# Dealing the rows of a weight to the partitions in another order, and its small vector with it

## Chip, cores, metric

One core of a Trainium2 chip. The metric is the device time of one execution in microseconds (us). All arithmetic and all data are float32.

## The reference

The kernel is one decode step (one token for each of two batch rows, D = 512) of a transformer block with adaptive layer norm. Cut to what matters here:

```python
mod = (silu(c) @ w_mod).reshape(2, 6, 1, 512)        # c: (2, 512), w_mod: (512, 3072)
sa, ca, ga, sb, cb, gb = six rows of mod
h = layernorm(x) * (1 + ca) + sa                     # x: (2, 1, 512)
x = x + ga * attention(h)                            # wq: (512, 4096), 8 kv heads, last 4096 of 32768 keys
h = layernorm(x) * (1 + cb) + sb
x = x + gb * (silu(h @ w1) @ w2)
```

The product of `silu(c)` with `w_mod` comes first: all that follows needs it, the query projection included. It sums over the 512 rows of `w_mod`. In which order they are summed, and which row lies in which partition, is free as long as `c` is dealt in the same order.

## The kernel before

**Memory.** All large operands are read once, in the order in which they are used, through one ring of eight slots of 16 KB in each partition (`slots`, function `stream`). A transfer takes one or more slots, and its issue has to wait until the work that read the former contents is done. All large transfers are issued by SyncE (SP) and so lie in one hardware queue, in this order: `w_mod` (three slots), `x`, `wq` (four slots), then for eight steps a pair of heads of the key cache and of the value cache (two slots each), then `wo`, `w1` and `w2`. The first pair of the key cache and the second take the slots of `w_mod` and one that has not been used, so SP issues them when the last matmuls on `w_mod` are done.

**`w_mod`.** `load_runs(w_mod, 4, 0, 4)` puts rows 4p to 4p+3 into partition p: each partition reads 48 KB that lie together in memory, and 128 such blocks make up the matrix.

**`c`.** The condition vector lies in the tile `xc` (half `c_sp`, 128 partitions by 128 elements, set to zero first). For each of the two batch rows the 512 numbers are cut into four pieces of 128, and each piece goes to the first or the 17th partition of a group of 32. ScalarE (ACT) issues four transfers for it, each with two pieces of 512 bytes, in a hardware queue of its own. VectorE (DVE) then transposes it in blocks of 32 by 32 (`turned`, line 255), which gives `cT`: partition r of step k holds element 4r + k. `silu_exp` and a product make `scT` out of it.

**The head of the kernel, in order.** DVE: zero `xc`, transpose `c` (this waits for the four transfers), SiLU, then small constants, then the layer norm's statistics of `x`, the modulated `h_a`, and its transpose `hq_T`. PE: 64 matmuls into `m_a` and `m_sp` (lines 269 and 272) with `scT` as weights and `w_mod` as data; then 64 matmuls of the query projection `q` (line 302) on `wq`; then the steps of the attention. Every engine works through its own list in order, so what stands behind the transpose of `c` on DVE waits with it.

**Steps of the attention.** In each step DVE transposes a pair of key heads (line 361), PE makes the scores (line 374), softmax follows, and PE weighs the values (line 448). SP issues the next transfers as slots come free (line 82).

Of the kernel before, what the change touches and what calls it, by code (L numbers as in the profile page):

```python
# [13 lines left out]
P = 128  # L14
B, D = 2, 512
# [8 lines left out]
def adaln_block(  # L24
# [19 lines left out]
    nc = tc.nc  # L44
# [16 lines left out]
    def const(shape, name):  # L61
        return consts.tile(shape, F32, name=name)

    def bank(tag, name):
        return (psum1 if tag in "CO" else psum).tile([P, 512], F32, tag=tag, name=name)
# [4 lines left out]
    def stream(n=1):  # L70
        i = turn_of[0]
        if n % 2 == 0:
            i += -i % n
        turn_of[0] = i + n
        return slots[:, i % RING : i % RING + n, :].rearrange("p s e -> p (s e)")
# [12 lines left out]
    def load_runs(w, per, lo, hi):  # L88

        e = w.shape[1]  # L90
        n = -(-(hi - lo) * e // 4096)
        t = stream(n)[:, : (hi - lo) * e].rearrange("p (q e) -> p q e", e=e)
        nc.sync.dma_start(t, w.rearrange("(p q) e -> p q e", q=per)[:, lo:hi, :])
        return t
# [3 lines left out]
    xc = const([P, 2, P], "xc")  # L98
    x_sp, c_sp = xc[:, 0, :], xc[:, 1, :]
    nc.vector.memset(xc, 0.0)  # L100
    wm = load_runs(w_mod, 4, 0, 4)
    rows8 = lambda t: t.rearrange("(ab r) m -> ab r m", r=16)[:, 0, :]
    for b in range(B):
        for lo in (0, 2):
            nc.scalar.dma_start(
                c_sp.rearrange("(g y) m -> g y m", g=4)[lo : lo + 2, 16 * b, :],
                c[b].rearrange("(g m) -> g m", m=P)[lo : lo + 2],
            )
    nc.sync.dma_start(rows8(x_sp), x2.rearrange("b (g m) -> g b m", m=P))  # L109
    wqt = load_runs(wq, 4, 0, 4)  # L110
# [108 lines left out]
    def silu_exp(t, name, shape):  # L219

        e = once.tile(shape, F32, tag="silu", name=name)
        nc.vector.tensor_scalar(e, t, -1.0, 87.0, op0=ALU.mult, op1=ALU.min)
        nc.scalar.activation(e, e, AF.Exp)
        nc.vector.tensor_scalar(e, e, 1.0, None, op0=ALU.add)
        nc.vector.reciprocal(e, e)
        return e
# [26 lines left out]
    def turned(t, name):  # L253
        o = const([P, 4, 32], name)
        nc.vector.transpose(o, t.rearrange("p (m k) -> p k m", k=4))  # L255
        return o

    cT = turned(c_sp, "cT")
    sg = silu_exp(cT, "sgc", [P, 4, 32])
    scT = const([P, 4, 32], "scT")  # L260
    nc.vector.tensor_mul(scT, cT, sg)  # L261
# [315 lines left out]
    for q in range(28):  # L577
        g = q % 4
# [80 lines left out]
    for tt in range(WIDE):  # L659
        g = tt % 4  # L660
# [7 lines left out]
    y = bank("D", "acc_y")[:, :P]  # L668
# [13 lines left out]
    for tt in range(11, T2):  # L682
        for h in range(2):
            for g in range(4):
                lo = g * P + h * H
# [46 lines left out]
```

## Time and profile before

| What | Value |
|---|---|
| median of 3 runs | 235.59 us (235.44 to 235.62) |
| the profiled execution | span of 233.7 us from its first to its last instruction; 1.9 us of the median lie outside it |
| busy: PE, DVE, ACT, POOL | 161.1, 115.6, 28.5, 10.5 us |
| read from memory | 97.53 MB, 417 GB/s over the span |
| packets of SP's queue | 3768, 97.1% of 16 engines' span |
| packets of ACT's queue | 16 |

Times in rows of the trace are in us from the span's start. In a row of the timeline stand start, duration, engine, line, operation, output and inputs; an "SPq" or "ACTq" row is the issue of a transfer, not the transfer itself. A view of the transfers by window gives, for that window, how many packets started, how many of them were under 512 bytes, and how many belonged to each queue: q1 is SP's, q10 is ACT's. The DMA share is the mean busy share of the 16 DMA engines; in a short window it can pass 1.00, since a packet counts where it starts.

### The profile page before, as it was taken

The page shows a single profiled execution, that of the slowest core. Times are in us where ns is not written, and L with a number is a line of the kernel's source. Part 1 is how long each engine was busy: PE and PEld are TensorE (multiplying, and loading weights), DVE is VectorE, ACT ScalarE, POOL GpSimd, SP SyncE. Part 2 cuts the span into 40 slices and gives each one's busy share as a digit, 9 for nine tenths or more (in the row PEclk, how much of TensorE's full clock was granted, in tenths as well). Part 3 has the DMA queues.
Part 4 walks back from the last instruction along what each step waited for, and adds up shares of the span by engine and source line. Part 5 has one row for each costly group of instructions (what it writes and reads, how often), then busy time and mean ns, then how long its engine had stood idle before and what let it go on. Part 6 is the DMA issues. An engine that isn't in the chain of part 4 may idle for free.

```text
span 233.7 us, 2571 instructions
## 1 busy us (share of the span) xinstructions
PE 161.1 (69%) x1070; PEld 43.3 (19%) x1070; DVE 115.6 (49%) x179; ACT 28.5 (12%) x64; POOL 10.5 (4%) x35
## 2 busy tenths in 40 slices
PE   0004916859577839797598749759759779789684
PEld 0001401201111111211120201202112122324222
DVE  0007240278894758695197089259559540101232
ACT  2000210000311120120210201111020120102020
POOL 2004710000000000000000000000000000000000
PEclk9999985979999977999979999988997997999999
DMA  7998998999999999999999999999999999989991
GB/s 269 446 542 359 404 494 359 446 444 421 415 421 449 446 437 415 426 426 446 449 437 409 418 437 449 449 421 412 426 444 449 443 421 437 463 367 437 424 404 57
DMA packets 3794, 97.68 MB, mean 418 GB/s; under 512 B 432, under 2 KB 456, under 8 KB 968
## 3 DMA queue, kind: packets, MB, share of 16 engines
q1 hardware_dynamic: 3768, 97.53, 97.1%
q8 instruction: 8, 0.13, 0.2%
q14 instruction: 2, 0.02, 0.0%
q10 hardware_dynamic: 16, 0.00, 0.0%
HBM read 97.53 MB, written 0.00 MB: 417 GB/s over the span
## 4 chain that ended last, share of the span: by engine, by line
DMA 60%; issue 18%; DVE 14%; PE 6%; POOL 0%; SPq 0%; POOLq 0%; ACT 0%
DMA slots<-in_A_k_cache_dram 22%; DMA slots<-in_A_wq_dram 15%; DMA slots<-in_A_v_cache_dram 12%; DMA slots<-in_B_w_dram 12%; DVE kT L361 11%; PE o L448 2%; PE q L302 2%; DVE zp L420 1%; PE acc_yw L661 1%; DVE xp L418 1%; PE qr L323 0%; PE acc_y L671 0%; DVE qT L315 0%; POOL qg L319 0%; SPq L109 0%
## 5 line engine op out<-in xcount | busy, mean ns | idle before, releaser
L361 DVE STREAM_TRANSPOSE kT<-slots 128x1024 f32<-128x1024 f32 x64 | 73.7, 1212 | 23.7 <-DMA slots<-in_A_k_cache_dram 23.6
L374 PE MATMUL s<-kT,qbd 128*32 128x512 f32 x256 | 68.6, 693 | 19.1 <-DVE kT L361 18.0
L448 PE MATMUL o<-slots,ptb 128*32 128x512 f32 x256 | 30.8, 624 | 2.1 <-DMA slots<-in_A_v_cache_dram 2.1
L374 PEld LDWEIGHTS s<-kT,qbd 128*32 128x32 f32 x256 | 9.6, 113 | 68.4 <-DVE kT L361 63.4
L269 PE MATMUL m_a<-slots,scT 128*32 128x256 f32 x32 | 4.4, 506 | 20.5 <-DVE scT L261 20.5
L302 PE MATMUL q<-slots,hq_T 128*32 128x512 f32 x64 | 8.3, 680 | 7.0 <-DMA slots<-in_A_wq_dram 7.0
L448 PEld LDWEIGHTS o<-slots,ptb 128*32 128x32 f32 x256 | 8.1, 114 | 17.9 <-issue 17.8
L404 ACT COPY bias<-bp 128x1 f32<-128x1 f32 x8 | 1.3, 159 | 77.0 <-PE bp L402 77.0
L384 DVE TENSOR_REDUCE mx<-s 128x1 f32<-128x512 f32 x8 | 5.5, 691 | 9.6 <-PE s L374 9.6
L565 PE MATMUL junk<-quad,id 128*32 128x512 f32 x22 | 10.2, 595 | 0.0
L420 DVE TENSOR_TENSOR zp<-xp,quarter 128x1024 f32<-128x1024 f32 x8 | 9.8, 1225 | 0.2
L435 ACT ACTIVATE ptb<-pT,odd 128x256 f32<-128x256 f32 x16 | 6.7, 472 | 25.6 <-PE pT L427 25.6
L255 DVE STREAM_TRANSPOSE cT<-xc 128x128 f32<-128x128 f32 x1 | 0.4, 401 | 16.7 <-DMA xc<-in_c_dram 16.7
L427 PE MATMUL pT<-zp,mix 128*32 128x256 f32 x64 | 5.7, 428 | 3.6 <-DVE zp L420 3.5
L458 ACT COPY ob<-o 128x512 f32<-128x512 f32 x8 | 4.7, 585 | 26.1 <-PE o L448 26.1
L272 PE MATMUL m_sp<-slots,scT 128*32 128x512 f32 x32 | 7.4, 738 | 0.0
L386 PE MATMUL mT<-ident,mx 128*1 128x128 f32 x16 | 3.0, 270 | 6.3 <-DVE mx L384 6.3
L315 DVE STREAM_TRANSPOSE qT<-q 128x512 f32<-128x512 f32 x2 | 1.4, 717 | 11.7 <-PE q L302 10.2
L418 DVE STREAM_TRANSPOSE xp<-pr 128x512 f32<-128x512 f32 x8 | 5.5, 686 | 3.4 <-ACT pr L406 3.4
L579 PE MATMUL acc_o<-slots,oTn 128*32 128x512 f32 x56 | 6.2, 593 | 0.7 <-DMA slots<-in_A_wo_dram 0.7
L466 PE MATMUL o_all<-ob,selh 128*64 128x128 f32 x64 | 6.0, 316 | 0.8 <-ACT ob L458 0.8
L550 DVE COPY acc_o_sb<-acc_o 128x256 f32<-128x256 f32 x1 | 0.4, 425 | 12.4 <-ACT acc_o_sb L549 12.4
(140 smaller groups left out, 93.8 us busy)
## 6 DMA issues: line engine op xcount, KB each, us to landing
slots<-in_A_k_cache_dram SPq DMA_DIRECT2D x8, 4096.0 KB, 27.4
slots<-in_A_v_cache_dram SPq DMA_DIRECT2D x8, 4096.0 KB, 27.6
slots<-in_w_mod_dram SPq DMA_DIRECT2D x1, 6144.0 KB, 17.1
slots<-in_A_wo_dram SPq DMA_DIRECT2D x1, 6144.0 KB
slots<-in_B_w_dram SPq DMA_DIRECT2D x1, 2688.0 KB
slots<-in_A_wo_dram SPq DMA_DIRECT2D x1, 2048.0 KB, 29.5
slots<-in_B_w_dram SPq DMA_DIRECT2D x1, 2048.0 KB
slots<-in_B_w_dram SPq DMA_DIRECT2D x1, 896.0 KB
```

The lines of the kernel that those rows point to most:

```text
L272: nc.tensor.matmul(m_sp[r, :], scT[:, k, :], cd[:, g], start=(k == 0), stop=(k == 3))
L302: nc.tensor.matmul(q_ps[n][32 * g : 32 * g + 32, :], hq_T[:, k, :], wv[:, n, g], start=(k == 0), stop=(k == 3),)
L361: inorder(nc.vector.transpose(kT[s, j][:, 32 * c : 32 * c + 32, :], kt[s].rearrange("p (n j r) -> p j n r", j=4, r=32)[:, j, 32 * c : 32 * ...
L374: inorder(nc.tensor.matmul(s_ps[s][r : r + 32, :], qbd[h // 4][:, h % 4, b, j, :], kT[s, j][:, 32 * c : 32 * c + 32, e:32:2], start=(j == ...
L418: inorder(nc.vector.transpose(xp, pr[s]))
L420: inorder(nc.vector.tensor_mul(zp, xp[:, None, :, 0:16].to_broadcast([P, 4, 16, 16]), quarter[:, :, None, None].to_broadcast([P, 4, 16, 16 ...
L427: inorder(nc.tensor.matmul(tp[32 * i : 32 * i + 32, :], mix.rearrange("p v e -> p (v e)"), zp.rearrange("p y t x -> p (y t) x")[:, :, 4 * ...
L435: inorder(nc.scalar.activation(ptb[s % 2][:, :, e, :], tp.rearrange("p (w z) -> p w z", z=16), AF.Copy, scale=odd[:, e : e + 1],))
L448: inorder(nc.tensor.matmul(o_ps[s][r : r + 32, :], ptb[s % 2][:, w].rearrange("p e z -> p (e z)"), vt[s].rearrange("p (c w m f d) -> p c f ...
L466: inorder(nc.tensor.matmul(o_all[r : r + 64, :], selh[:, m, lo : lo + 2 * HQ], o_sb[s][:, m * DH : (m + 1) * DH], start=(s == 0 and m < 2) ...
L565: inorder(nc.tensor.matmul(junk[0:32, :], id4, quad.rearrange("p m y -> p (m y)"), start=True, stop=True,))
L579: inorder(nc.tensor.matmul(acc[32 * g : 32 * g + 32, :], oTn[:, q, :], wot[q], start=(q < 4), stop=(q >= 24),))
```

## The change

Partition 8j + i now receives block 16i + j of `w_mod` (a block is four rows, 48 KB), for i below 8 and j below 16; before, partition p received block p. `c` has to follow: what was one run of 128 numbers for a partition becomes eight runs of 16, each from another place of the vector. The four transfers of `c` stay four, with the same destinations, and so does the number of bytes. The transpose of `c` reads its tile in a permuted order, so that `cT` matches the new rows. Nothing else is touched: on every engine the same instructions follow each other in the same order.

```diff
-    wm = load_runs(w_mod, 4, 0, 4)
+    wm = stream(3)[:, : 24 * D].rearrange("p (q e) -> p q e", e=6 * D)
+    nc.sync.dma_start(
+        wm.rearrange("p q e -> p (q e)"),
+        w_mod.rearrange("(i j q) e -> j i (q e)", i=8, j=16),
+    )
     rows8 = lambda t: t.rearrange("(ab r) m -> ab r m", r=16)[:, 0, :]
     for b in range(B):
         for lo in (0, 2):
             nc.scalar.dma_start(
-                c_sp.rearrange("(g y) m -> g y m", g=4)[lo : lo + 2, 16 * b, :],
-                c[b].rearrange("(g m) -> g m", m=P)[lo : lo + 2],
+                c_sp.rearrange("(g y) (i a) -> g y i a", g=4, i=8)[lo : lo + 2, 16 * b],
+                c[b].rearrange("(i g a) -> g i a", i=8, g=4)[lo : lo + 2],
             )
...
-    cT = turned(c_sp, "cT")
+    cT = const([P, 4, 32], "cT")
+    nc.vector.transpose(
+        cT.rearrange("p k (y i) -> p k y i", i=8),
+        c_sp.rearrange("p (i y k) -> p k y i", y=4, k=4),
+    )
```

## The prediction, made before the changed kernel ran

> **What bounds the kernel now.** I read the page first: its slices, its queues, and the costliest groups.
>
> ```profile
> span 233.7 us, 2571 instructions
> ...
> q1 hardware_dynamic: 3768, 97.53, 97.1%
> ...
> q10 hardware_dynamic: 16, 0.00, 0.0%
> ...
> L255 DVE STREAM_TRANSPOSE cT<-xc 128x128 f32<-128x128 f32 x1 | 0.4, 401 | 16.7 <-DMA xc<-in_c_dram 16.7
> ...
> slots<-in_w_mod_dram SPq DMA_DIRECT2D x1, 6144.0 KB, 17.1
> ```
>
> SP's queue keeps the 16 DMA engines busy for 97.1% of the span, and it carries all bytes that matter. So the time is the length of that queue plus what stands before and behind it. The windows of the whole kernel (the last two columns are DMA share and GB/s) show whether it ever runs dry:
>
> ```profile
> 6.00:18.00 12.00, 0.00 (x0) 0.00 (x0) 0.12 (x1) 0.00 (x0) 0.00 (x0) 1.00 1.11 481
> 18.00:37.00 19.00, 9.81 (x68) 3.34 (x68) 7.96 (x31) 2.44 (x4) 7.94 (x23) 0.90 0.96 414
> 37.00:77.00 40.00, 30.47 (x166) 6.76 (x170) 23.96 (x29) 4.51 (x11) 0.47 (x2) 0.92 1.00 432
> 77.00:117.00 40.00, 29.55 (x186) 7.05 (x178) 27.06 (x33) 5.82 (x15) 0.49 (x2) 0.91 1.00 432
> 117.00:157.00 40.00, 30.18 (x173) 6.64 (x173) 25.36 (x29) 4.72 (x12) 0.00 (x0) 0.94 1.00 432
> 157.00:197.00 40.00, 32.48 (x206) 8.66 (x208) 24.18 (x30) 5.37 (x14) 0.00 (x0) 0.89 1.02 437
> 197.00:228.00 31.00, 26.17 (x202) 9.11 (x194) 5.04 (x22) 4.01 (x6) 0.00 (x0) 1.00 0.97 416
> ```
>
> It doesn't: the share is 1.00 within the rounding of packets from 6 us to 228 us. Two things follow. A microsecond in which this queue stands empty is lost for good, as no later stage has slack to win it back. And there is little rate to gain while it is full. So the question is whether the change makes the queue faster, or makes it run dry. What could make it run dry is in the head, in the timeline:
>
> ```profile
> 0.73 0.38 SPq L93 DMA_DIRECT2D slots<-in_w_mod_dram  x1
> ...
> 1.16 2.62 ACTq L105 DMA_DIRECT2D xc<-in_c_dram  x4
> ...
> 1.93 0.58 SPq L93 DMA_DIRECT2D slots<-in_A_wq_dram  x1
> ...
> 17.88 0.40 DVE L255 STREAM_TRANSPOSE cT<-xc 128x128 f32<-128x128 f32 x1 [16.75 <-DMA xc<-in_c_dram]
> ...
> 20.51 1.08 PE L269 MATMUL m_a<-slots,scT 128*32 128x256 f32 x8 [20.51 <-DVE scT L261]
> ...
> 29.08 1.84 SPq L82 DMA_DIRECT2D slots<-in_A_k_cache_dram  x2
> ...
> 30.69 0.40 DVE L255 STREAM_TRANSPOSE hq_T<-h_a 128x128 f32<-128x128 f32 x1
> ...
> 37.29 8.34 PE L302 MATMUL q<-slots,hq_T 128*32 128x512 f32 x64 [6.97 <-DMA slots<-in_A_wq_dram]
> ```
>
> The four transfers of `c`, 4 KB in all, are issued by 3.78 and are seen at 17.88: 14 us for 4 KB. From there runs a chain: SiLU, the matmuls on `w_mod`, their slots come free, and SP issues the first key transfers at 29.08. `wq` lands at 37.16 (issued at 1.93, 35.23 us on the chain of waits); until then the queue lives on `wq`.
>
> ```profile
> 1.93 35.23 DMA slots<-in_A_wq_dram
> 37.15 0.14 issue
> ```
>
> So `c` has a slack of about 8 us before the queue runs dry. Why `c` takes 14 us is seen in the transfers by window, here from 6.0 to 7.9, from 7.9 to 9.7, from 9.7 to 11.5 and from 17.0 to 17.6 us:
>
> ```profile
> DMA packets 20, 0.89 MB, mean 466 GB/s; under 512 B 0, under 2 KB 2, under 8 KB 2
> ...
> q10 hardware_dynamic: 2, 0.00, 0.2%
> ...
> DMA packets 18, 0.79 MB, mean 437 GB/s; under 512 B 2, under 2 KB 2, under 8 KB 2
> ...
> q10 hardware_dynamic: 2, 0.00, 0.1%
> ...
> DMA packets 17, 0.74 MB, mean 410 GB/s; under 512 B 0, under 2 KB 2, under 8 KB 2
> ...
> q10 hardware_dynamic: 2, 0.00, 0.2%
> ...
> DMA packets 44, 0.92 MB, mean 1538 GB/s; under 512 B 20, under 2 KB 30, under 8 KB 30
> ...
> q10 hardware_dynamic: 4, 0.00, 0.8%
> ```
>
> ACT's queue gets two packets in each 1.8 us, and their sizes alternate: two of 512 bytes, then two under 512 bytes, then two of 512 bytes. I read this as two engines that take one packet of `c` after each 48 KB packet of `w_mod`: first a data packet, a turn later the packet that reports the completion. Sixteen packets are eight data runs and eight completions, so a transfer of two runs goes to two engines with one run each, and a run is a packet. Eight turns at 1.8 us are the 14 us.
>
> **The change part by part.** *The runs of `c`.* Each transfer has two partitions as before, hence two engines, but eight runs of 64 bytes for each. An engine gets 4 x (8 + 1) = 36 packets instead of 8. By one packet for each turn, 6 go beside the `w_mod` packets until 17.0, 1 to 4 beside the small packets of 17.0 to 17.6 (completion of `w_mod`, `x`), 8 beside the `wq` packets (64 KB, eight for each engine) and 1 beside the completion of `wq`. That makes 16 to 19. The other 17 to 20 find SP's queue empty and run through alone. So `c` lands when `wq` has landed, plus a remainder: 37.16 in place of 17.88.
>
> The remainder: two packets took 0.2% of 16 engines in 1.9 us, which is 0.06 us, so 0.03 us for each. About 12 more of them than before lie in front of the end of `wq` (0.36 us), and about 18 behind it (0.55 us). The lower bound is nothing; as upper bound I take 0.1 us for each behind it (1.8 us), since in the last window the four packets of `c` pass beside others within 0.6 us. I take the row's 0.03, which is for the same queue.
>
> *The issue of `w_mod`.* Its source pattern gets one level more, like that of the key cache, whose issues take longer in the rows of the tile `slots` up to 50 us (min/median/max in ns):
>
> ```profile
> L82 SPq DMA_DIRECT2D slots<-in_A_k_cache_dram x3: 535/546/599, 29.1 to 45.7; - x3
> L93 SPq DMA_DIRECT2D slots<-in_w_mod_dram x1: 377/377/377, 0.7 to 0.7; - x1
> ```
>
> That is +0.16 us on the start of the queue (bounds: 0 and 0.22), and nothing hides it.
>
> *The order of the reads.* The queue already moves 432 GB/s where it is full, and `w_mod` moves at that pace but for its start. `wq` (8192 KB) lands 19.33 us behind `w_mod` (0.73 + 17.1 = 17.83), which is 2.36 us for 1024 KB; by that pace the 6144 KB of `w_mod` need 14.5 us of its 17.1. The other 2.6 us are what a transfer into an empty queue costs before and behind its bytes. All that another order can save lies in there. The first sixteen packets, one for each engine, start between 1.7 and 3.0 us:
>
> ```profile
> DMA packets 16, 0.79 MB, mean 605 GB/s; under 512 B 0, under 2 KB 0, under 8 KB 0
> ```
>
> So about 1.0 of the 2.6 pass before any packet, whatever the order. Taken as 0; bounds: a gain of 1.6 us and, the other way, a start as much worse.
>
> *The transpose of `c`.* Same 128x128 elements, one level more in the source: 0.40 us, taken as unchanged; bounds: 0 and 0.4 us more, should the level double it.
>
> *The sum.* `cT` starts at 37.16 + 0.16 + 0.36 + 0.55 = 38.2 in place of 17.88, 20.3 us later. Nothing on DVE, PE or POOL can go ahead of it: the constants, the statistics of `x` and the matmuls all stand behind it or need it. So the 11.2 us from 17.88 to the issue at 29.08 follow unchanged and SP issues the keys at 49.4. This transfer now meets an empty queue and pays the 2.6 us, plus 0.16 which its issue takes longer than that of `w_mod`: 49.4 + 2.76 = 52.2. Before, its bytes followed those of `wq` directly, from 37.16. The queue has lost 52.2 - 37.16 = 15.0 us, and all of it reaches the end. The span has 233.7 us against the median of 235.59; the 1.9 us outside it stay. 235.59 + 15.0 = 250.6 us.
>
> What lies beside it: `hq_T` starts at 30.69 + 20.3 = 51.0 and `q` ends some 9 us behind, at about 60, while the first keys land at 52.2 + 9.4 (4096 KB at 2.36) = 61.6. `q` stays hidden, and `wq`'s slots come free before the queue, which by then holds two pairs of keys, is done with them. If `q` were later by 2 us, the scores would start late, but the queue would not notice.
>
> **The rivals.** *Several runs in one turn.* If an engine takes all that one `c` transfer has for it in a turn, `c` costs no more turns than before. The threshold is low: the queue runs dry only if the key issue comes after 37.16 - 2.76 = 34.4, so `cT` after 23.2. With three packets in a turn, 36 packets need 12 turns, which end with the second `wq` packet at about 17.4 + 2 x 2.4 = 22.2 (16 packets of `wq` in 19.33 / 8 = 2.4 us): just no loss. With two, 18 turns end with `wq` all the same. The time then is 235.59 + 0.16 = 235.75. Against it speaks that a data packet and its own completion, which lie behind one another in the same queue, took turns 1.8 us apart. [...]
>
> *Faster: the new order pays at the start.* If neighbouring blocks end the slow start of `w_mod`, and `c` isn't late, the queue ends earlier by up to 1.6 - 0.16 = 1.4 us; half of it gives 234.9. It decides only together with the first rival, since a queue that waits for `c` gains nothing from an earlier `w_mod`. The full rate of 432 GB/s from 37 us on, with the key cache read in its own order, speaks against a large part.
>
> *The remainder is dear.* If each of the 18 lone packets takes 0.1 us, `cT` starts 1.25 us later: 251.9.
>
> **How the numbers follow.** 0.2% of the time, 0.47 us, is about what can be told from no change. I give the forecast 0.86, the dear remainder 0.03, several runs in a turn 0.07 (of which 0.06 within 0.2% and 0.01 faster by luck of the start), and the faster start with it 0.04. So: faster 0.05, same 0.06, slower 0.89. The range stays with the slow cases, since the others hold only 0.11. Its lower end takes no remainder and no small packets in front (-0.9), and 1.0 instead of 2.6 us for the empty queue (-1.6), with some more for a head that runs faster while the DMA engines are idle: 247.8. Its upper end takes the dear remainder, 0.4 for the transpose and some for the start: 252.6.
>
> **What would show it.** In the changed kernel's profile the DMA slices drop to nothing for one or two slices of 5.84 us at about 38 to 51 us; ACT's queue shows 72 packets in place of 16, two in each 1.8 us and then in each 2.4 us; `cT` starts at about 38 and the idle time before it is about 37 us on `c`; SP issues the first keys at about 49. The forecast is wrong if `cT` still starts near 18 us, and its size is wrong if the empty stretch isn't near 15 us or if a later window makes up for it.

## The result, and the profile after

The changed kernel takes 264.3 us (median; 263.94 to 265.5) against 235.58 us (235.35 to 235.62) of the kernel before, run beside it: a ratio of 1.1237, 95% interval 1.122 to 1.1254. The sign was right, the size was not: 250.6 us had been forecast, in a range up to 252.6. The loss is 28.7 us in place of 15.0. The profile is of the run of 265.5 us.

The page of the changed kernel shows two lean stretches at the start, where one had been expected:

```profile
span 263.7 us, 2571 instructions
...
DMA  9899979700999999999999999999999999989992
GB/s 209 172 216 239 279 318 477 318 0 25 385 462 399 467 408 432 435 432 442 418 450 408 462 413 445 423 427 447 418 455 409 447 423 460 447 370 430 431 418 101
...
q10 hardware_dynamic: 72, 0.00, 0.0%
...
L263 DVE STREAM_TRANSPOSE cT<-xc 128x128 f32<-128x128 f32 x1 | 0.4, 394 | 52.1 <-DMA xc<-in_c_dram 52.1
...
slots<-in_w_mod_dram SPq DMA_DIRECT2D x1, 6144.0 KB, 33.1
```

A slice is 6.6 us here. Slices 9 and 10 hold almost no transfer: that is the empty queue of the forecast. But the first five slices are busy and still move only 172 to 279 GB/s, and `w_mod` lands 33.1 us after its issue, not 17.1. A DMA share near 1 beside half the rate means that each packet takes twice as long; a share alone would have hidden it. The windows (share and GB/s are the last two columns) set the stages apart, first `w_mod`, then `wq`, then the empty queue, then all the rest up to 226 us:

```profile
6.00:30.00 24.00, 0.00 (x0) 0.00 (x0) 0.00 (x0) 0.00 (x0) 0.00 (x0) 1.00 1.01 211
34.00:52.00 18.00, 0.00 (x0) 0.00 (x0) 0.00 (x0) 0.00 (x0) 0.00 (x0) 1.00 0.94 408
53.00:65.00 12.00, 9.18 (x65) 3.37 (x68) 5.76 (x24) 1.85 (x3) 7.21 (x21) 1.00 0.00 0
66.00:226.00 160.00, 121.22 (x728) 28.06 (x732) 101.99 (x123) 20.78 (x53) 1.70 (x6) 0.91 1.00 431
```

At 211 GB/s a 48 KB packet takes 3.7 us on each of 16 engines; the trace's packets of `w_mod` behind the first round have 3.54 to 3.85 us, before the change nearly all 1.815. From 66 us on the kernel runs at its old rate, so nothing is won back. The timeline shows the head:

```profile
0.73 0.69 SPq L102 DMA_DIRECT2D slots<-in_w_mod_dram  x1
...
53.19 0.39 DVE L263 STREAM_TRANSPOSE cT<-xc 128x128 f32<-128x128 f32 x1 [52.06 <-DMA xc<-in_c_dram]
...
55.82 1.08 PE L277 MATMUL m_a<-slots,scT 128*32 128x256 f32 x8 [55.82 <-DVE scT L269]
...
64.49 1.84 SPq L82 DMA_DIRECT2D slots<-in_A_k_cache_dram  x2
...
66.56 7.07 PE L310 MATMUL q<-slots,hq_T 128*32 128x512 f32 x64 [0.83 <-DVE hq_T L259]
```

`c` is seen 49.3 us after its last issue (at 3.91), and the chain of waits now leads through it instead of through `wq`:

```profile
3.39 49.68 DMA xc<-in_c_dram
```

How the 72 packets of `c` went is in the transfers by window, from 9 to 32, 32 to 33, 34 to 52 and 52 to 53 us:

```profile
q10 hardware_dynamic: 12, 0.00, 0.1%
...
q10 hardware_dynamic: 10, 0.00, 0.9%
...
q10 hardware_dynamic: 14, 0.00, 0.1%
...
q10 hardware_dynamic: 36, 0.00, 2.4%
```

That is 6 turns for each of two engines beside `w_mod`, 5 beside small packets, 7 beside `wq` (an eighth falls into the last window), and the rest in a row once SP's queue is empty. That is the count of the forecast, turn by turn, with 5 beside the small packets where it had 1 to 4. What the forecast had not seen is the half rate of `w_mod`.

### The profile page after: what moved, and what is told of

Read it like the earlier page. It is cut to its first block, busy times and chain, and to the rows that moved or that the text cites. A ratio compares the mean times of both kernels' runs of the same rounds, so it can differ in the third digit from the quotient of the medians.

```text
span 263.7 us, 2571 instructions
## 1 busy us (share of the span) xinstructions
PE 160.9 (61%) x1070; PEld 42.8 (16%) x1070; DVE 115.6 (44%) x179; ACT 28.5 (11%) x64; POOL 10.5 (4%) x35
## 2 busy tenths in 40 slices
DMA packets 3850, 97.68 MB, mean 370 GB/s; under 512 B 496, under 2 KB 512, under 8 KB 1024
## 4 chain that ended last, share of the span: by engine, by line
DMA 60%; issue 17%; DVE 13%; PE 8%; ACTq 1%; POOL 0%; ACT 0%; POOLq 0%; DVEq 0%
DMA slots<-in_A_k_cache_dram 19%; DMA xc<-in_c_dram 19%; DMA slots<-in_B_w_dram 11%; DMA slots<-in_A_v_cache_dram 11%; DVE kT L369 10%; PE m_sp L280 2%; PE q L310 1%; PE o L456 1%; PE m_a L277 1%; DVE zp L428 1%; ACTq L109 1%; PE acc_yw L669 1%; DVE xp L426 0%; DVE sgc L229 0%; PE acc_y L679 0%
## 5 line engine op out<-in xcount | busy, mean ns | idle before, releaser
L382 PE MATMUL s<-kT,qbd 128*32 128x512 f32 x256 | 70.5, 731 | 20.6 <-DVE kT L369 19.7
L456 PE MATMUL o<-slots,ptb 128*32 128x512 f32 x256 | 29.1, 595 | 2.3 <-DMA slots<-in_A_v_cache_dram 2.3
L277 PEld LDWEIGHTS m_a<-slots,scT 128*32 128x32 f32 x32 | 1.2, 125 | 56.6 <-DVE scT L269 55.8
L587 PE MATMUL acc_o<-slots,oTn 128*32 128x512 f32 x56 | 7.9, 727 | 2.3 <-DMA slots<-in_A_wo_dram 2.3
L310 PE MATMUL q<-slots,hq_T 128*32 128x512 f32 x64 | 7.1, 594 | 0.8 <-DVE hq_T L259 0.8
L558 DVE COPY acc_o_sb<-acc_o 128x256 f32<-128x256 f32 x1 | 0.4, 425 | 15.8 <-ACT acc_o_sb L557 15.8
L474 PE MATMUL o_all<-ob,selh 128*64 128x128 f32 x64 | 5.4, 290 | 0.8 <-ACT ob L466 0.8
## 6 DMA issues: line engine op xcount, KB each, us to landing
slots<-in_w_mod_dram SPq DMA_DIRECT2D x1, 6144.0 KB, 33.1
```

What stands on the lines that cost most here:

```text
L277: nc.tensor.matmul(m_a[r, :], scT[:, k, :], ab[:, g], start=(k == 0), stop=(k == 3))
L310: nc.tensor.matmul(q_ps[n][32 * g : 32 * g + 32, :], hq_T[:, k, :], wv[:, n, g], start=(k == 0), stop=(k == 3),)
L382: inorder(nc.tensor.matmul(s_ps[s][r : r + 32, :], qbd[h // 4][:, h % 4, b, j, :], kT[s, j][:, 32 * c : 32 * c + 32, e:32:2], start=(j == ...
L456: inorder(nc.tensor.matmul(o_ps[s][r : r + 32, :], ptb[s % 2][:, w].rearrange("p e z -> p (e z)"), vt[s].rearrange("p (c w m f d) -> p c f ...
L587: inorder(nc.tensor.matmul(acc[32 * g : 32 * g + 32, :], oTn[:, q, :], wot[q], start=(q < 4), stop=(q >= 24),))
```

## The experiments

**One half of the change: `w_mod` alone.** `c` and its transpose stay as they were, so the numbers of `c` meet other rows.

```diff
-    wm = load_runs(w_mod, 4, 0, 4)
+    wm = stream(3)[:, : 24 * D].rearrange("p (q e) -> p q e", e=6 * D)
+    nc.sync.dma_start(wm.rearrange("p q e -> p (q e)"),
+        w_mod.rearrange("(i j q) e -> j i (q e)", i=8, j=16))
```

> Half of the change: w_mod in the new order, c and its transpose as before (so the numbers of c meet other rows of w_mod than they should; every instruction keeps its size). If the 28.7 us are two separate terms, a slow w_mod and a late c, this run has the first alone: its 48 KB packets take 3.8 us as in the changed kernel, w_mod lands near 33.5 us, c keeps its 8 turns and is seen at about the same time, the first keys are issued near 45 us, before wq lands near 53 us, so the queue never runs dry, and the time is 235.6 + 15.7 = 251.3 (250.5 to 252). Rival: the eight short runs of c also slow the w_mod packets of all engines; then the packets here take 1.8 us and the time is near 236.

Measured: 251.3 us (251.15 to 251.37) against 235.51, ratio 1.067 (1.0654 to 1.0686). Its window from 6 to 30 us and its timeline:

```profile
6.00:30.00 24.00, 0.00 (x0) 0.00 (x0) 0.00 (x0) 0.00 (x0) 0.00 (x0) 1.00 1.00 207
```

```profile
33.42 0.40 DVE L259 STREAM_TRANSPOSE cT<-xc 128x128 f32<-128x128 f32 x1 [32.29 <-DMA xc<-in_c_dram]
43.33 1.84 SPq L82 DMA_DIRECT2D slots<-in_A_k_cache_dram  x2
```

The new order alone halves the rate and costs 15.8 us. `c` with its eight turns is as early as `w_mod`, and the keys are issued at 43.33, before the last packets of `wq` end at 52.7 us, so the queue never runs dry.

**The other half: `c` in eight runs.** `w_mod` and the transpose as before.

```diff
-                c_sp.rearrange("(g y) m -> g y m", g=4)[lo : lo + 2, 16 * b, :],
-                c[b].rearrange("(g m) -> g m", m=P)[lo : lo + 2],
+                c_sp.rearrange("(g y) (i a) -> g y i a", g=4, i=8)[lo : lo + 2, 16 * b],
+                c[b].rearrange("(i g a) -> g i a", i=8, g=4)[lo : lo + 2],
```

> The other half: c in eight runs for a partition, w_mod and the transpose of c as before (so again c meets other rows). If an engine takes one packet of c in a turn, c has 36 packets for each of two engines and lands just behind wq: the transpose of c starts near 37.5 us, the first keys are issued near 48.7 us, the queue stands empty for about 14 us, and the time is 235.6 + 14.3 = 249.9 (249.3 to 250.6). Rival: c was late in the changed kernel only because w_mod was slow and c waited for it; then c is seen near 18 us and the time is 235.6.

Measured: 248.92 us (248.18 to 249.44), ratio 1.0568 (1.0543 to 1.0593): 13.4 us, which is 0.4 below the range expected for this run. The profile is of the run of 248.18 us. The timeline, and the window in which the queue is empty:

```profile
37.16 0.40 DVE L255 STREAM_TRANSPOSE cT<-xc 128x128 f32<-128x128 f32 x1 [36.03 <-DMA xc<-in_c_dram]
47.45 1.83 SPq L82 DMA_DIRECT2D slots<-in_A_k_cache_dram  x2
```

```profile
37.00:48.00 11.00, 8.21 (x65) 3.27 (x68) 5.82 (x24) 1.85 (x3) 7.21 (x21) 1.00 0.00 0
```

This is the forecast's mechanism by itself: the last packets of `c` go when their engines are through with `wq`, and the queue stands empty until the keys are issued. The two halves make 15.8 + 13.4 = 29.2 us, the whole change 28.7: they add up within the spread of the runs, since the empty queue comes behind the slow `w_mod` and not beside it.

**Two and four runs of `c`.** The same edit with `i=2` and with `i=4`.

> w_mod as before the change, c in two runs of 64 numbers for a partition (so its numbers meet other rows of w_mod). An engine has 12 packets of c in place of 8, or of 36 with eight runs. Theory of turns: 6 pass beside w_mod, 3 or 4 beside the small packets behind it, 2 or 3 beside the first packets of wq; the transpose of c starts at 20 to 24 us, the first keys are issued at 31 to 35 us, while wq still runs until 37, and the time is that of before, 235.3 to 235.9. Rival (each further run costs alike): a seventh of the 13.4 us that seven further runs cost, 1.9 us, so 237.4.

> w_mod as before the change, c in four runs of 32 numbers for a partition (its numbers meet other rows of w_mod). An engine has 20 packets of c. Theory of turns: 6 beside w_mod, 3 or 4 beside small packets, 8 beside wq, the last few behind wq: as late as with eight runs, the transpose of c near 37, time 248.3 to 249.3. Rival (each further run costs alike): three sevenths of 13.4 us, 241.3.

Measured: 235.46 us with two runs (ratio 0.9993, 0.9983 to 1.0002) and 248.48 us with four (ratio 1.0552, 1.0534 to 1.057). The timelines, two runs first:

```profile
20.07 0.40 DVE L255 STREAM_TRANSPOSE cT<-xc 128x128 f32<-128x128 f32 x1 [18.95 <-DMA xc<-in_c_dram]
30.96 1.84 SPq L82 DMA_DIRECT2D slots<-in_A_k_cache_dram  x2
```

```profile
37.47 0.40 DVE L255 STREAM_TRANSPOSE cT<-xc 128x128 f32<-128x128 f32 x1 [36.34 <-DMA xc<-in_c_dram]
47.47 1.84 SPq L82 DMA_DIRECT2D slots<-in_A_k_cache_dram  x2
```

Two runs cost nothing and four cost as much as eight. A price for each run can't do that; turns can. With two runs an engine has twelve packets of `c`, and the last starts at 19.6 us, early in `wq`. With four it has twenty, and the last starts at 36.8 us, when the packets of `wq` end.

**Why is `w_mod` slow: reads or writes?** Two kernels separate what the change did at once. In one, `w_mod` is dealt as 32 by 4, so blocks that follow each other on the source's outermost level still lie side by side in memory, but the outermost count is 32. In the other the source stays 16 by 8, but its blocks lie 9 apart on that level, in the key cache (6144 KB of it stand in for `w_mod`). In both, `c` is as before. The edits are shown against the kernel with `w_mod` alone.

```diff
-        w_mod.rearrange("(i j q) e -> j i (q e)", i=8, j=16))
+        w_mod.rearrange("(i j q) e -> j i (q e)", i=4, j=32))
```

```diff
-        w_mod.rearrange("(i j q) e -> j i (q e)", i=8, j=16))
+        k_cache[0, 0].rearrange("s d -> (s d)")[: 16 * 9 * 24 * D]
+            .rearrange("(j i e) -> j i e", j=16, i=9)[:, :8, :])
```

> w_mod dealt as 32 by 4 instead of 16 by 8: partition 4j+i receives block 32i+j (i below 4, j below 32); c as before, so it meets other rows. The engines still read neighbouring blocks at a time. Theory of the reads (neighbouring 48 KB blocks are slow to read): packets again take 3 to 3.8 us, time 247 to 252. [...]

> A source of 16 by 8 blocks of 48 KB that do not neighbour each other: 6144 KB of the key cache in place of w_mod (so the result is of other data), partition 8j+i receives block 9j+i, so the engines read 432 KB apart, nearly as before the change (384 KB). c as before. Theory of the reads: packets take 1.815 us, time 235.6 to 236.3. [...]

Measured: 235.94 us for 32 by 4 (ratio 1.0022, 1.0012 to 1.0032) and 251.82 us for the far blocks (ratio 1.0693, 1.0675 to 1.0711). The windows, 6 to 16 us of 32 by 4, then 6 to 30 us of the far blocks:

```profile
6.00:16.00 10.00, 0.00 (x0) 0.00 (x0) 0.00 (x0) 0.00 (x0) 0.00 (x0) 1.00 1.01 438
```

```profile
6.00:30.00 24.00, 0.00 (x0) 0.00 (x0) 0.00 (x0) 0.00 (x0) 0.00 (x0) 1.00 1.03 213
```

The theory of the reads had it the other way round. What lies side by side doesn't set the rate: with 16 outermost, near blocks run at 207 GB/s and far ones at 213, and with 32 outermost near blocks run at 438. The outermost count made the difference. (The 384 and 432 KB in the text above suppose that an engine takes eight neighbouring partitions. No run shows how any of these loads is dealt to the engines, and the comparison doesn't need it.) The 32 by 4 form is 0.43 us slower than before, and this is its issue and start:

```profile
0.73 0.65 SPq L102 DMA_DIRECT2D slots<-in_w_mod_dram  x1
```

It takes 0.65 us against 0.38, and `w_mod` lands 17.8 us after its start in place of 17.1.

**Where the engines write.** It was my guess that with 16 outermost the 16 engines write at one time to partitions 8 apart, and that the places written slow each other; no run shows how that load is dealt. Three kernels load `w_mod` as eight transfers of 16 partitions, so the partitions that one transfer writes are known: 8 apart, neighbours, or 7 apart. Each transfer has sixteen packets of 48 KB, and a DMA share of 0.96 to 1.04 says that all engines are at work. Each partition gets its rows of before.

```diff
-    wm = load_runs(w_mod, 4, 0, 4)
+    wm = stream(3)[:, : 24 * D].rearrange("p (q e) -> p q e", e=6 * D)
+    wmf = wm.rearrange("p q e -> p (q e)")
+    wsrc = w_mod.rearrange("(p q) e -> p (q e)", q=4)
+    for i in range(8):     # 8 apart; neighbours: [16 * i : 16 * i + 16] of both
+        nc.sync.dma_start(wmf.rearrange("(j i) e -> i j e", i=8)[i],
+            wsrc.rearrange("(j i) e -> i j e", i=8)[i])
```

> w_mod as eight transfers of 16 partitions each, partitions i, i+8, ..., i+120 in transfer i; every partition gets the same rows as before the change, and c is as before, so the result is the reference's. Each engine has one 48 KB packet of each transfer, and at a time the sixteen engines write to partitions 8 apart, as I suppose they do in the changed kernel. [...] Rival (only the three-level source is slow, not the places written): 1.815 us, 236 to 237.

> The same with 16 neighbouring partitions in each transfer (16i to 16i+15), result the reference's. [...] Rival (a transfer cut into sixteen parts runs at half rate, wherever it writes): packets of 3.8 us, time 251 to 252.5. Rival (only the three-level source is slow): 236 to 237.

> The same with seven transfers of 16 partitions that are 7 apart (o, o+7, ..., o+105) and one of the last 16 neighbours; result the reference's. [...] Rival (half rate for any cut into sixteen): 251 to 252.5. Rival (only the three-level source): 236 to 237.

Measured, in two runs each: 252.23 us for 8 apart, 276.61 us for neighbours, 251.85 us for 7 apart (ratios 1.0701, 1.0679 to 1.0722; 1.1735, 1.1709 to 1.1762; 1.0685, 1.0663 to 1.0706). The windows in that order:

```profile
6.00:30.00 24.00, 0.00 (x0) 0.00 (x0) 3.77 (x15) 0.31 (x1) 4.51 (x17) 1.00 1.04 215
```

```profile
8.00:56.00 48.00, 0.00 (x0) 0.00 (x0) 3.76 (x15) 0.31 (x1) 7.21 (x21) 1.00 0.97 110
```

```profile
6.00:24.00 18.00, 0.00 (x0) 0.00 (x0) 3.62 (x15) 0.31 (x1) 1.18 (x6) 1.00 0.96 232
```

8 apart repeats the changed kernel's rate (215 GB/s beside 211), packet for packet 3.81 us. Neighbours run at 110 GB/s, a quarter of the 438 of the 32 by 4 form, with packets of 6.93 us. The rival that only a three-level source is slow (236 to 237 us) fell in all three, as their sources have two levels. They also part writes from reads: neighbours read 16 blocks that lie together, as the changed kernel does if engine j gets piece j, and run at half of its rate; 8 apart read blocks 384 KB apart and run at its rate.

With 7 apart, nearly all packets of the seven transfers behind the first round took 2.1 to 3.7 us, and none 1.8. The time of 251.85 us lies in the range of the rival of half the rate for any cut into sixteen; against that rival stand the neighbours' 110 GB/s. So the rate goes with the partitions that are written together, but by which rule they slow each other these three runs don't show.

**Eight engines at a time.** Three more kernels take 8 partitions for each transfer, which uses eight engines (a DMA share of 0.46 to 0.52 in their first windows) and leaves room. The loop is the same with 8 rows; the partitions of a transfer lie 4 apart and then 12 apart (`96+o+4j`, then `o+12j`), 8 apart from 0 and from 64 on, or 8 apart from 40 on, then 3 and 5 apart. The triples of the loop are shown for the first kernel; for the second they are `(0, 64, 8), (64, 128, 8)`, and for the third `(40, 104, 8), (104, 128, 3), (0, 40, 5)`.

```diff
+    for lo, hi, s in ((96, 128, 4), (0, 96, 12)):
+        for i in range((hi - lo) // 8):
+            base = lo + 8 * s * (i // s)
+            part = lambda t: t[base : base + 8 * s].rearrange("(j o) e -> o j e", o=s)[i % s]
+            nc.sync.dma_start(part(wmf), part(wsrc))
```

> w_mod as sixteen transfers of 8 partitions each, which use eight engines; each partition gets the same rows as before the change and the result is the reference's. [...]

> [...]

> [...]

Measured, in two runs each: 258.92, 291.5 and 274.54 us (ratios 1.0994, 1.2378, 1.1657). The windows show where the packets keep their pace and where they don't. First 4 and 12 apart, 5 to 23 and 26 to 38 us:

```profile
5.00:23.00 18.00, 0.00 (x0) 0.00 (x0) 3.76 (x15) 0.72 (x2) 7.21 (x21) 1.00 0.46 200
26.00:38.00 12.00, 0.00 (x0) 0.00 (x0) 0.00 (x0) 0.00 (x0) 0.00 (x0) 1.00 0.87 186
```

then 8 apart from 0 and 64 on, 6 to 40 us, and 8 apart from 40 on, 5 to 17 us:

```profile
6.00:40.00 34.00, 0.00 (x0) 0.00 (x0) 3.76 (x15) 0.31 (x1) 7.20 (x21) 1.00 0.52 109
```

```profile
5.00:17.00 12.00, 0.00 (x0) 0.00 (x0) 3.77 (x15) 0.96 (x2) 2.76 (x12) 1.00 0.49 185
```

Until `wq` starts, 4 and 12 apart lose nothing: all packets behind the first round take 1.815 us. With 8 apart from 0 and 64 on, most take 3.8 us. With 8 apart from 40 on, two packets of eight take 3.84 us and six 1.815; six at 49152 bytes / 1.815 us and two at 49152 bytes / 3.84 us make 188 GB/s, and the window has 185. So the distance alone doesn't decide: 8 apart runs at 109 GB/s to one set of partitions and at 185 to another, with blocks 384 KB apart in memory both times.

Later the pace falls. In the first two kernels the other eight engines had nothing to do in `w_mod` and went on to `wq` (from 23.9 us in the first, from 42.3 us in the second). From there the packets of the remaining transfers took 3.3 to 3.7 us in the first kernel and 5.1 to 5.5 in the second. Why isn't shown: no run shows which partitions these eight engines write.

In the third kernel SP issues `wq` only at 36.73 us, so eight engines work alone until then. Yet the rate falls long before, when the second group of transfers, 3 apart, begins:

```profile
17.00:24.00 7.00, 0.00 (x0) 0.00 (x0) 0.00 (x0) 0.00 (x0) 4.44 (x10) 1.00 0.50 119
...
36.73 0.36 SPq L93 DMA_DIRECT2D slots<-in_A_wq_dram  x1
```

The packets of 48 KB of this group that start in the window took 2.7 to 3.7 us (share and rate make 3.3 in the mean); none kept 1.815. That is the riddle of 7 apart again, with eight engines in place of sixteen: with 8 apart from 40 on six packets of eight kept 1.815 us, with 3 apart and 7 apart none did behind the first round. What these have in common isn't shown by these runs and stays open.

## Why the prediction was right or wrong, point by point

**The bound.** Right. The queue is the time: it is full before, and after the change it is full but for the one empty stretch, and what it lost in the head came out at the end.

**The runs of `c`.** Right in mechanism, a little too dear. The late `c` alone cost 13.4 us, forecast 15.0. In the profiled run `cT` started at 37.16 in place of 38.2. Of this, 0.16 us belong to the issue of `w_mod`, which this run leaves as it was. The rest is the remainder of 0.36 + 0.55 us, which hardly shows: the two engines that carry `c` were through with `wq` at 36.33, before the last packet of `wq` ended on another engine at 36.95, and the lone packets followed each other at about 7 ns. The 30 ns of the forecast were read from packets of 512 bytes; in the changed kernel those of 64 bytes took 18 to 24 ns beside `w_mod` and 11 ns beside `wq`. The chain from `cT` to the key issue took 10.3 us, not 11.2; in the runs that load `w_mod` in one transfer it took 9.9 to 11.3, and why it varies isn't shown. The rival of several runs in one turn fell: beside `w_mod` and `wq` each of the two engines took one packet of ACT's queue for each turn of 3.8 or 2.4 us in the changed kernel, even where nine of a transfer stood ready.

**The order of the reads: the step that failed.** The prediction wrote that the queue moves at 432 GB/s where it is full, that only 2.6 us at the start could change, "taken as 0", with a bound of 1.6 us either way. The term measured 15.8 us with `w_mod` alone, about 0.4 of it the longer issue. The rows were right, but they were rows of transfers that are cut otherwise. The bound assumed that another source pattern changes only which addresses are read; it also changed the outermost count, and with it, as the runs of 16 partitions suggest but don't show for this load, where sixteen engines write at one moment. I argued about reads and never asked about writes, though the new pattern was on the page of the change: 16 outermost (207 GB/s) where the key cache has 64 (432, caches together, from 37 to 77 us) and the old form 128 (472 at a share of 1.09). A bound of "as much worse" was taken from nothing.

**Two slips in the working.** `wq` at 19.33 us for 8192 KB makes 2.42 us for 1024 KB, not 2.36; the 14.5 us for `w_mod` go by 2.42, and only the landing of the first keys would be 0.2 us later, which the sum doesn't use. And the slack of about 8 us leaves out the 2.76 us that the keys pay in an empty queue; by the threshold of 23.2 us that the rival names, it is 5.3 us.

**The issue of `w_mod`.** Right sign, too small: 0.16 us from the key cache's issue of 0.54. The first issue of the kernel took 0.65 to 0.70, and the 32 by 4 kernel, which has this term alone, lost 0.43 us.

**The transpose of `c`.** Right: 0.39 us in place of 0.40.

**Faster through neighbouring reads.** Fell: near blocks ran at 438 GB/s with a share of 1.01 in the 32 by 4 kernel, before at 472 with 1.09, which is the same 433 for a share of 1, with a first round no faster than before (packets of 2.2 to 3.0 us, before 1.9 to 3.0), and nothing gained.

**What was worth trying for a faster kernel** had nothing to find: the 32 by 4 form was 0.43 us slower than before, and the queue was full there already.

## What to carry to other kernels

When an access pattern of a load changes, ask for both sides what the engines do at one moment: here an outermost count of 16 ran a 128-partition load at 207 to 213 GB/s, where counts of 32 and 128 ran at 433 for a full share, and the caches with 64 at 432. Read the DMA share and the GB/s together, since a share of 1.01 at 211 GB/s is a slow transfer and not a full one. And count the packets of a small transfer beside a large one: here each waited for one packet of the other queue, so twelve were free, twenty cost 13 us, and the price lies in the turn at which the next large issue comes too late.

## What the runs showed of the hardware that I had not expected

- A load of 6144 KB with 16 by 8 source pieces ran at 207 to 213 GB/s, with near blocks and far ones; 32 by 4 ran at 438. With transfers of sixteen neighbouring partitions it ran at 110.
- With eight engines at work, the time of a 48 KB packet went with the partitions written together: 1.815 us for 4 and 12 apart, mostly 3.8 for 8 apart from 0 and 64 on, 3.84 for two of eight and 1.815 for six with 8 apart from 40 on, 2.7 to 3.7 for 3 apart. With sixteen engines it was 3.81 us for 8 apart, 6.93 for neighbours, 2.1 to 3.7 for 7 apart. This is measured and not explained.
- Alone, packets of 64 bytes passed at about 7 to 9 ns each on an engine; beside a queue of 48 KB or 64 KB packets each waited 1.8, 2.4 or 3.8 us, the length of the packet ahead.
